# Attention with one ones-matmul for two units' row sums, and an x ring of six batches

## The chip, the cores and the metric

One core of one Trainium2 chip. The metric is device time in microseconds (us), the median over several executions. The kernel before takes about 1066 us. In its first runs its executions agreed within 0.1%, but over all rounds they lie between 1063.2 and 1068.4 us, a scatter of about 0.5%; so differences of 1 or 2 us need care. Ratios are the mean time of one kernel's fast runs over that of the other's of the same rounds, so not quite the ratio of the medians quoted beside them.

## The reference, cut to what matters

Two independent attention problems, A and B, of the same shape; their outputs are concatenated.

```python
# per problem: x (16, 144, 448), k_cache and v_cache (16, 16, 512, 256), wq (448, 4096), wo (4096, 448), bf16
q = (x @ wq).reshape(B, Sq, H, Dh).transpose(0, 2, 1, 3)
scores = einsum("bhqd,bhkd->bhqk", q, k_cache) * Dh ** -0.5
p = softmax(scores, axis=-1)
o = einsum("bhqk,bhkd->bhqd", p, v_cache)
out = o.transpose(0, 2, 1, 3).reshape(B, Sq, H * Dh) @ wo
```

A *unit* is one (problem, batch, head): 512 units, each with 144 queries and 512 keys. Units 0 to 255 are problem A, 256 to 511 problem B.

## The kernel before

The scores are kept transposed: keys lie on the partitions, queries on the free axis. So the softmax sum over the keys runs over partitions, and TensorE does it: GpSimd adds the four key blocks elementwise to a tile of 128x144, and a matmul with a 128x128 tile of ones sums that tile over its partitions and puts the sum on all 128 partitions. ScalarE turns the sum into a reciprocal as exp(-ln(sum)).

```python
def t_sum(U):                                  # every unit
    t.matmul(ot_ps[ob][:, 2*SQ:3*SQ], lhsT=ones[:, :], rhs=ps_sb[:, U % NPS, :], start=True, stop=True)
def t_recip(U):
    a.activation(ln, ot_ps[ob][:, 2*SQ:3*SQ], AF.Ln)
    a.activation(rinv_sb[:, sl, :], ln, AF.Exp, scale=-1.0)
def t_check(U):                                # a guard: max and min of the sums
    v.tensor_reduce(run_sb[0:1, k, j:j+1], ot_ps[ob][0:1, 2*SQ:3*SQ], ...)   # k = max, min
# ... (cut)
# one step i of the program; every engine gets its instructions in this order
t_q(i + LQ); t_evac_q(i + LQ)    # Q projection of a unit ahead (often two batches in one), copied by VectorE
t_s(i + LS)                      # scores; ScalarE's exponentials
t_pv(i); t_sum(i)                # P.V and the ones-matmul
t_presum(i + LS)                 # GpSimd's adds
t_recip(i); t_check(i)
t_evac_ot(i)                     # VectorE: P.V times reciprocal -> ring
# ... output projection pieces ("OP"), two matmuls of 448 columns at a time
```

Every load is issued by one queue (SyncE), in a fixed order: V two units at a time into nine slots, K sixteen units at a time by a transposing DMA into two slots ("K block 16" is units 256 to 271), x by a transposing DMA. The first 48 units take their K in natural layout and are transposed by TensorE, with the old sum form in both kernels.

Of the kernel before, what the change touches and what calls it, by code (L numbers as in the profile page):

```python
# [752 lines left out]
def bass_concat_heads__mha_block_cached__gqa_block_cached__near_ridge_kernel(  # L753
# [22 lines left out]
    NP = 2  # L776
# [16 lines left out]
    LQ, LS, LT = 3, 2, 4  # L793
    KW, KR = 16, 32
    NV, NXG = 9, 2
    NNAT = 3 * KW // UV
    assert KR % KW == 0 and NU % KW == 0
    XB = 4
    assert Bn % (NXG * XB) == 0 and H == KW
    NQT, NPT, NPS, NRI, NOST, NRUN = 11, 3, 2, 2, 2, 32  # L800
# [3 lines left out]
    NXGT = NP * Bn // XB  # L804
# [12 lines left out]
    with contextlib.ExitStack() as es:  # L817
# [13 lines left out]
        xt_sb = sb("xt_sb", [128, 4, NXG * XB * SQ], BF16)  # L831
# [6 lines left out]
        run_sb = sb("run_sb", [1, 2, NRUN], BF16)  # L838
        runs_sb = sb("runs_sb", [1, 2, NT // NRUN], F32)
# [17 lines left out]
        for i in range(NXG):  # L857
            sem_names.append("xt%d" % i)
# [8 lines left out]
        def unit(U):  # L867
            pr, r = divmod(U, NU)
            b, h = divmod(r, H)
            return pr, b, h  # L870

# [43 lines left out]
        def t_load_x(XG):  # L915
            pr, j = divmod(XG, Bn // XB)
            sl = XG % NXG
            c0 = sl * XB * SQ
            x = xs[pr][j * XB:(j + 1) * XB].rearrange("b q d -> (b q) d")

            def e(q):
                q.dma_start_transpose(xt_sb[:, 0:3, c0:c0 + XB * SQ], x[:, 0:384]).then_inc(sems["xt%d" % sl], 16)  # L922
                return q.dma_start_transpose(xt_sb[:, 3, c0:c0 + XB * SQ], x[:, 320:448]).then_inc(sems["xt%d" % sl], 16)  # L923
            S.add(SP, e, writes=[(("xt", sl), XG)], dma_sem="xt%d" % sl, n_dma=2, name="x%d" % XG)
# [59 lines left out]
        def q_pair(U):  # L984

            b, h = unit(U)[1:]
            if U < NNAT * UV:
                return 1
            if U < NNAT * UV + H and h % 2 == 0:
                return 1  # L990
            if h % 2 == 0:
                return 2 if b % 2 == 0 else 0
            j = b % (NXG * XB)
            return 1 if j in (0, NXG * XB - 1) else (2 if j % 2 else 0)
# [3 lines left out]
        for U in range(NT):  # L998
            for u in [u for u in q_live if u - LS < U - LQ]:
                del q_live[u]  # L1000
            free = [k for k in range(NQT) if k not in q_live.values()][:q_pair(U)]
            for k, sl in enumerate(free):
                q_slot[U + k * H] = q_live[U + k * H] = sl

        def t_q(U):
            pr, b, h = unit(U)
            n = q_pair(U)
            xo = b % (NXG * XB) * SQ
            xr = sorted(set((pr * Bn + b + k) // XB for k in range(n)))
            hg = h // 4  # L1010

            def e(t):
                ins = None
                for dc in range(2):
                    for kc in range(4):
                        c0 = h * DH + dc * 128
                        acc = qp_ps[:, dc, 0:2 * SQ] if n == 2 else qp_ps[:, 0, dc * SQ:(dc + 1) * SQ]
                        ins = t.matmul(acc, lhsT=wq_sb[:, kc, c0:c0 + 128],  # L1018
                                       rhs=xt_sb[:, kc, xo:xo + n * SQ], start=(kc == 0), stop=(kc == 3))
                return ins  # L1020
            S.add(PE, e, reads=[(("wq", hg), pr), ("wqz", 0)] + [(("xt", XG % NXG), XG) for XG in xr],
                  writes=[(bk, ("q", U)) for bk in q_banks[:n]], banks=q_banks[:n], name="Q%d" % U)

        def t_evac_q(U):
            n = q_pair(U)
            us = [U + k * H for k in range(n)]
            a, b = q_slot[us[0]], q_slot[us[-1]]

            def e(v):
                if n == 1:  # L1030
                    return v.tensor_copy(qt_sb[:, a, :, :], qp_ps[:, 0, 0:2 * SQ].rearrange("p (e q) -> p e q", e=2))  # L1031
                return v.tensor_copy(qt_sb[:, a:b + 1:b - a, :, :],  # L1032
                                     qp_ps[:, :, 0:2 * SQ].rearrange("p e (u q) -> p u e q", u=2))
            S.add(DVE, e, reads=[(bk, ("q", U)) for bk in q_banks[:n]],
                  writes=[(("qt", q_slot[u]), u) for u in us], banks=q_banks[:n],
                  name="eq%d" % U)

        def t_s(U):
# [4 lines left out]
            kn = [(("ktn", U % KR), U)] if U < NNAT * UV else []  # L1043
            psl = U % NPT
            for k in range(2):
                bank = k if U < NNAT * UV else (2 * U + k) % 3
# [11 lines left out]
            for k in range(2):  # L1058
                bank = k if U < NNAT * UV else (2 * U + k) % 3

                def x(a, k=k, bank=bank):
                    return a.activation(pt_sb[:, psl, 2 * k:2 * k + 2, :].rearrange("p b q -> p (b q)"),  # L1062
                                        s_ps[bank][:, 0:2 * SQ], AF.Exp, scale=DH ** -0.5)
                S.add(ACT, x, reads=[(("sp", bank), 2 * U + k)], writes=[(("pt", psl), U)], banks=["s%d" % bank],
                      name="ex%d.%d" % (U, k))

        def t_presum(U):
# [5 lines left out]
            S.add(POOL, e1, reads=[(("pt", psl), U)], writes=[("pp", U)], name="pp%d" % U)  # L1073

            def e2(g):
                return g.tensor_tensor(ps_sb[:, sl, :], pp_sb[:, 0, :], pp_sb[:, 1, :], op=ALU.add)  # L1076
            S.add(POOL, e2, reads=[("pp", U)], writes=[(("ps", sl), U)], name="ps%d" % U)
# [26 lines left out]
        def t_sum(U):  # L1104
            sl = U % NPS
            ob = U % 2

            def e(t):
                return t.matmul(ot_ps[ob][:, 2 * SQ:3 * SQ], lhsT=ones[:, :], rhs=ps_sb[:, sl, :],  # L1109
                                start=True, stop=True)  # L1110
            S.add(PE, e, reads=[("ones", 0), (("ps", sl), U)], writes=[(("sum", ob), U)],
                  banks=["ot%d" % ob], name="SM%d" % U)

        def t_recip(U):
            ob = U % 2
            sl = U % NRI
            ln = rinv_sb[:, sl, :]

            def e1(a):
                return a.activation(ln, ot_ps[ob][:, 2 * SQ:3 * SQ], AF.Ln)  # L1120
            S.add(ACT, e1, reads=[(("sum", ob), U)], writes=[(("rinv", sl), (U, 0))], banks=["ot%d" % ob],
                  name="ln%d" % U)

            def e2(a):
                return a.activation(rinv_sb[:, sl, :], ln, AF.Exp, scale=-1.0)  # L1125
            S.add(ACT, e2, reads=[(("rinv", sl), (U, 0))], writes=[(("rinv", sl), U)], name="rc%d" % U)
# [22 lines left out]
        def t_check(U):  # L1149
            ob = U % 2  # L1150
            j = U % NRUN
            for k, op in ((0, ALU.max), (1, ALU.min)):
                def e(v, k=k, op=op):
                    return v.tensor_reduce(run_sb[0:1, k, j:j + 1], ot_ps[ob][0:1, 2 * SQ:3 * SQ], axis=AX.X, op=op)  # L1154
                S.add(DVE, e, reads=[(("sum", ob), U)], writes=[(("run", k), U // NRUN)], banks=["ot%d" % ob],
                      name="ck%d.%d" % (U, k))
            if j == NRUN - 1:
                for k, op in ((0, ALU.max), (1, ALU.min)):
                    def e(v, k=k, op=op):
                        return v.tensor_reduce(runs_sb[0:1, k, U // NRUN:U // NRUN + 1], run_sb[0:1, k, :],  # L1160
                                               axis=AX.X, op=op)
                    S.add(DVE, e, reads=[(("run", k), U // NRUN)], writes=[(("runs", k), 0)],
                          name="cr%d.%d" % (U, k))

        def t_flag():
            for k, op in ((0, ALU.max), (1, ALU.min)):
                def e1(v, k=k, op=op):
                    return v.tensor_reduce(stat[0:1, 2 + k:3 + k], runs_sb[0:1, k, :], axis=AX.X, op=op)
                S.add(DVE, e1, reads=[(("runs", k), 0)], writes=[(("runx", k), 0)], name="runx%d" % k)

            def e2(v):
                return v.tensor_scalar(stat[0:1, 1:2], stat[0:1, 2:3], 2.0 ** LIM_EXP, None, op0=ALU.is_gt)
            S.add(DVE, e2, reads=[(("runx", 0), 0), ("scr1", 0)], writes=[("fl0", 0)], name="fl0")

            def e3(v):
                return v.scalar_tensor_tensor(flag_sb[0:1, 0:1], stat[0:1, 3:4], 2.0 ** -LIM_EXP, stat[0:1, 1:2],
                                              op0=ALU.is_lt, op1=ALU.max)
            return S.add(DVE, e3, reads=[(("runx", 1), 0), ("fl0", 0)], writes=[("flag", 0)], name="flag")
# [51 lines left out]
        s_min = -LQ - 24  # L1230
# [7 lines left out]

        for XG in range(1, NXGT):
            lo = (XG - NXG + 1) * XB * H - LQ if XG >= NXG else s_min  # L1240
            plan(lo, 0, t_load_x, XG)
        for W in range(NNAT * UV // KW, NKW):
            plan(KW * (W + 1) - KR - LS, 1, t_load_k, W)
# [21 lines left out]
        for fn, args in dma_plan:  # L1265
# [5 lines left out]
            elif fn is t_load_k:  # L1271
                lo = KW * (args[0] + 1) - KR - LS
            elif fn is t_load_x and args[0] >= NXG:
                lo = (args[0] - NXG + 1) * XB * H - LQ
            elif fn is t_load_wq and args[0]:
                lo = NU - H + 4 * args[1] + 4 - LQ
# [5 lines left out]
        qp_free = NT - LQ  # L1282
# [22 lines left out]
        while True:  # L1305
# [13 lines left out]
            if 0 <= u < NNAT * UV:  # L1319
                t_tr(u, 0)  # L1320
            u = i + LQ
            if 0 <= u < NT and q_pair(u):
                t_q(u)
                t_evac_q(u)
            u = i + LS
            if 0 <= u < NT:
                t_s(u)
            u = i + LT
            if 0 <= u < NNAT * UV:
                t_tr(u, 1)  # L1330
            if -LS <= i < 0:
                t_presum(i + LS)
            u = i
            if 0 <= u < NT:
                t_pv(u)
                t_sum(u)
                if u + LS < NT:
                    t_presum(u + LS)
                t_recip(u)
                t_check(u)  # L1340
# [42 lines left out]
        flag_ap = flag_sb[0:1, 0:1]  # L1383
# [72 lines left out]
```

## Time and profile before

1066.05 us (1065.64 to 1066.07, three runs). The profile is of another execution, which took 1063.18 us, 2.9 us less than that median; its span is 1061.4 us.

From the page of the kernel before: busy time, three of the rows of 40 slices, and the chain of work that ended last.

```profile
PE 1043.1 (98%) x12736; PEld 895.5 (84%) x12736; DVE 670.9 (63%) x2063; ACT 706.4 (67%) x2133; POOL 625.6 (59%) x1030
...
PE   6999999999999999999998999999999999999997
...
PEclk9999999999999999999998999999999999999999
DMA  9999999999999999999999999999999999999950
...
PE 97%; DMA 2%; SPq 1%; DVE 0%; issue 0%; ACT 0%; DVEq 0%
```

TensorE (PE) is busy nearly throughout and makes up 97% of the chain.

The groups that the change touches, by line and shape: busy us and mean ns of one, then the idle time of the engine just before them.

```profile
L1109 PE MATMUL ot_ps<-ps_sb,ones 128*128 128x144 bf16 x512 | 115.9, 226 | 0.0
...
L1154 DVE TENSOR_REDUCE run_sb<-ot_ps 1x1 bf16<-1x144 f32 x1024 | 262.3, 293 | 324.0 <-ACT rinv_sb L1120 324.0
...
L1120 ACT ACTIVATE rinv_sb<-ot_ps 128x144 f32<-128x144 f32 x512 | 150.1, 293 | 51.0 <-PE ot_ps L1109 8.0
...
L1125 ACT ACTIVATE rinv_sb<-rinv_sb 128x144 f32<-128x144 f32 x512 | 165.4, 323 | 16.1
```

A matmul's 226 ns is the length of its record, not its price. The price is the distance between starts, 62.5 ns here. Part of TensorE's timeline in mid-run (start us, duration, line, count):

```profile
501.27 1.14 PE L1018 MATMUL qp_ps<-xt_sb,wq_sb 128*128 128x288 bf16 x8
502.25 0.66 PE L1052 MATMUL s_ps<-qt_sb,kt_sb 128*128 128x144 bf16 x8
502.75 0.66 PE L1097 MATMUL ot_ps<-pt_sb,v_sb 128*128 128x144 bf16 x8
503.25 0.23 PE L1109 MATMUL ot_ps<-ps_sb,ones 128*128 128x144 bf16 x1
503.31 0.54 PE L1196 MATMUL op_ps<-wo_sb,ring 128*128 128x448 bf16 x2
```

Eight matmuls of 144 columns take 502.75 - 502.25 = 0.50 us, 62.5 ns each; the ones-matmul 0.06 us; eight of 288 columns 0.98 us. Over the whole trace the typical distances are 63, 123 and 189 ns for 144, 288 and 448 columns (56 ns for 128); columns/2.4 + 2.5 ns is a straight line fitted to them. This gives a yardstick: **lost time** is the sum, over successive matmuls, of the distance between starts beyond columns/2.4 + 2.5 ns (gaps of 8 ns or less are left out). Because a matmul is shown as 226 ns long but may be followed after 62 ns, a gap of up to 160 ns doesn't show as idle time at all; lost time sees it.

Who TensorE waited for, longest in total first (us in total, times, longest):

```profile
PE s_ps L972 <- DMA v_sb<-in_A_k_cache_dram: 6.1, 4, 4.7
PE qp_ps L1018 <- DMA xt_sb<-in_A_x_dram: 3.6, 1, 3.6
PE ot_ps L1097 <- DMA v_sb<-in_B_v_cache_dram: 3.0, 1, 3.0
PE op_ps L1196 <- DVE ring L1140: 0.4, 1, 0.4
```

The first two are the start, the third is one wait for V at the switch from A to B.

### The profile page before, as it was taken

To read this page: it belongs to the slowest core of one execution; us is meant where nothing else is said; L and a number is where in the kernel's file an instruction comes from. 1 tells how busy PE (TensorE), PEld (TensorE's weight loads), DVE (VectorE), ACT (ScalarE), POOL (GpSimd) and SP (SyncE) were. 2 spreads that over 40 slices of the span, in tenths; PEclk is the share of its full clock that TensorE was granted. 3 is DMA by queue.
4 is the path that set the end of the run, shared out by engine and by line. 5 is a ranking of instruction groups with operands and counts; after the bars stand their busy time and mean duration, and the time that the engine had idled before them with its cause. 6 is when DMAs were issued, how large, how long until landed. Compare 5 with 4: busy or idle time off the path is not lost.

```text
span 1061.4 us, 32383 instructions
## 1 busy us (share of the span) xinstructions
PE 1043.1 (98%) x12736; PEld 895.5 (84%) x12736; DVE 670.9 (63%) x2063; ACT 706.4 (67%) x2133; POOL 625.6 (59%) x1030
## 2 busy tenths in 40 slices
PE   6999999999999999999998999999999999999997
PEld 6999888888888888888887888888888888888885
DVE  4776666666666666666665666666666666666664
ACT  4887656667756666666855666676775666667674
POOL 3554555656656566666754656566665555666663
PEclk9999999999999999999998999999999999999999
DMA  9999999999999999999999999999999999999950
GB/s 304 379 350 285 295 293 254 274 297 273 292 276 298 208 280 267 290 292 298 262 287 352 265 274 290 291 290 301 264 263 265 304 285 289 289 290 279 239 187 13
DMA packets 588801, 294.15 MB, mean 277 GB/s; under 512 B 500576, under 2 KB 513376, under 8 KB 588640
## 3 DMA queue, kind: packets, MB, share of 16 engines
q1 hardware_dynamic: 588640, 291.99, 109.1%
q8 instruction: 102, 1.67, 0.6%
q14 instruction: 59, 0.48, 0.2%
HBM read 161.48 MB, written 4.13 MB: 156 GB/s over the span
## 4 chain that ended last, share of the span: by engine, by line
PE 97%; DMA 2%; SPq 1%; DVE 0%; issue 0%; ACT 0%; DVEq 0%
PE s_ps L1052 24%; PE ot_ps L1097 24%; PE qp_ps L1018 24%; PE op_ps L1196 20%; PE ot_ps L1109 3%; DMA v_sb<-in_A_k_cache_dram 1%; PE s_ps L972 1%; PE qp_ps L972 1%; PE qp_ps L1196 1%; DMA v_sb<-in_B_v_cache_dram 1%; SPq L922 0%; SPq L923 0%; DVE ost_sb L1217 0%; SPq L902 0%; DVE run_sb L1154 0%
## 5 line engine op out<-in xcount | busy, mean ns | idle before, releaser
L1072 POOL TENSOR_TENSOR pp_sb<-pt_sb 128x288 f32<-128x288 bf16 x512 | 374.0, 731 | 345.7 <-ACT pt_sb L1062 323.5
L1062 ACT ACTIVATE pt_sb<-s_ps 128x288 bf16<-128x288 f32 x1024 | 364.4, 408 | 268.5 <-PE s_ps L1052 268.0
L1154 DVE TENSOR_REDUCE run_sb<-ot_ps 1x1 bf16<-1x144 f32 x1024 | 262.3, 293 | 324.0 <-ACT rinv_sb L1120 324.0
L1097 PE MATMUL ot_ps<-pt_sb,v_sb 128*128 128x144 bf16 x4096 | 340.7, 226 | 3.0 <-DMA v_sb<-in_B_v_cache_dram 3.0
L1052 PE MATMUL s_ps<-qt_sb,kt_sb 128*128 128x144 bf16 x4096 | 340.8, 226 | 0.0
L1052 PEld LDWEIGHTS s_ps<-qt_sb,kt_sb 128*128 128x128 bf16 x4096 | 288.2, 98 | 43.5 <-DVE qt_sb L1032 0.2
L1018 PE MATMUL qp_ps<-xt_sb,wq_sb 128*128 128x288 bf16 (+1 forms) x2496 | 305.3, 266 | 3.6 <-DMA xt_sb<-in_A_x_dram 3.6
L1076 POOL TENSOR_TENSOR ps_sb<-pp_sb 128x144 bf16<-128x144 f32 x512 | 250.8, 490 | 76.2 <-PE ot_ps L1109 3.1
L1018 PEld LDWEIGHTS qp_ps<-xt_sb,wq_sb 128*128 128x128 bf16 x2496 | 218.8, 98 | 79.0 <-issue 4.4
L1196 PE MATMUL op_ps<-wo_sb,ring 128*128 128x448 bf16 x1120 | 285.0, 353 | 0.4 <-DVE ring L1140 0.4
L1097 PEld LDWEIGHTS ot_ps<-pt_sb,v_sb 128*128 128x128 bf16 x4096 | 274.6, 98 | 3.7 <-DMA v_sb<-in_B_v_cache_dram 3.2
L1140 DVE TENSOR_TENSOR ring<-ot_ps,rinv_sb 128x288 bf16<-128x288 f32 (+2 forms) x640 | 231.0, 375 | 0.0
L1120 ACT ACTIVATE rinv_sb<-ot_ps 128x144 f32<-128x144 f32 x512 | 150.1, 293 | 51.0 <-PE ot_ps L1109 8.0
L1032 DVE CAST qt_sb<-qp_ps 128x576 bf16<-128x576 f32 x200 | 151.1, 755 | 41.7 <-PE qp_ps L1018 37.6
L1125 ACT ACTIVATE rinv_sb<-rinv_sb 128x144 f32<-128x144 f32 x512 | 165.4, 323 | 16.1
L1109 PE MATMUL ot_ps<-ps_sb,ones 128*128 128x144 bf16 x512 | 115.9, 226 | 0.0
L1196 PEld LDWEIGHTS op_ps<-wo_sb,ring 128*128 128x128 bf16 x1120 | 94.0, 98 | 21.8 <-DVE ring L1140 0.8
L1031 DVE CAST qt_sb<-qp_ps 128x288 bf16<-128x288 f32 x112 | 49.2, 439 | 9.4 <-PE qp_ps L1018 8.8
L1109 PEld LDWEIGHTS ot_ps<-ps_sb,ones 128*128 128x128 bf16 x512 | 50.2, 98 | 0.0
L980 ACT ACTIVATE kt_sb<-qp_ps 128x512 bf16<-128x512 bf16 x48 | 28.9, 603 | 8.5 <-PE qp_ps L972 8.5
L972 PE MATMUL s_ps<-qt_sb,v_sb 128*128 128x128 bf16 x192 | 19.4, 226 | 6.2 <-DMA v_sb<-in_A_k_cache_dram 6.1
L980 DVE COPY kt_sb<-s_ps 128x512 bf16<-128x512 bf16 x48 | 19.5, 405 | 6.3 <-PE s_ps L972 6.2
(21 smaller groups left out, 85.1 us busy)
## 6 DMA issues: line engine op xcount, KB each, us to landing
v_sb<-in_A_v_cache_dram SPq DMA_DIRECT2D x128, 512.0 KB, 6.9
v_sb<-in_B_v_cache_dram SPq DMA_DIRECT2D x128, 512.0 KB, 7.1
v_sb<-in_A_k_cache_dram SPq DMA_DIRECT2D x24, 512.0 KB, 9.3
out_dram<-ost_sb SPq DMA_DIRECT2D x36, 112.0 KB, 6.1
wo_sb<-in_A_wo_dram SPq DMA_DIRECT2D x8, 448.0 KB, 8.5
wo_sb<-in_B_wo_dram SPq DMA_DIRECT2D x8, 448.0 KB, 8.9
wq_sb<-in_A_wq_dram SPq DMA_DIRECT2D x4, 768.0 KB, 9.2
wq_sb<-in_B_wq_dram SPq DMA_DIRECT2D x4, 768.0 KB, 10.1
```

Source lines behind the costliest of these rows:

```text
L1018: ins = t.matmul(acc, lhsT=wq_sb[:, kc, c0:c0 + 128], rhs=xt_sb[:, kc, xo:xo + n * SQ], start=(kc == 0), stop=(kc == 3))
L1032: return v.tensor_copy(qt_sb[:, a:b + 1:b - a, :, :], qp_ps[:, :, 0:2 * SQ].rearrange("p e (u q) -> p u e q", u=2))
L1052: ins = t.matmul(s_ps[bank][:, (c % 2) * SQ:(c % 2 + 1) * SQ], lhsT=kt_sb[:, 2 * c + dc, ko:ko + 128], rhs=qt_sb[:, qsl, dc, :], start=(dc ...
L1062: return a.activation(pt_sb[:, psl, 2 * k:2 * k + 2, :].rearrange("p b q -> p (b q)"), s_ps[bank][:, 0:2 * SQ], AF.Exp, scale=DH ** -0.5)
L1072: return g.tensor_tensor(pp_sb[:, :, :], pt_sb[:, psl, 0:2, :], pt_sb[:, psl, 2:4, :], op=ALU.add)
L1076: return g.tensor_tensor(ps_sb[:, sl, :], pp_sb[:, 0, :], pp_sb[:, 1, :], op=ALU.add)
L1097: ins = t.matmul(ot_ps[ob][:, dc * SQ:(dc + 1) * SQ], lhsT=v_sb[:, vsl, j, c * DH + dc * 128:c * DH + (dc + 1) * 128], rhs=pt_sb[:, sl, c, ...
L1109: return t.matmul(ot_ps[ob][:, 2 * SQ:3 * SQ], lhsT=ones[:, :], rhs=ps_sb[:, sl, :], start=True, stop=True)
L1125: return a.activation(rinv_sb[:, sl, :], ln, AF.Exp, scale=-1.0)
L1140: ins = v.tensor_tensor(ring[:, 2 * h:2 * h + 2, r0:r0 + q1 - q0], ot_ps[ob][:, 0:2 * SQ].rearrange("p (c q) -> p c q", c=2)[:, :, q0:q1], ...
L1154: return v.tensor_reduce(run_sb[0:1, k, j:j + 1], ot_ps[ob][0:1, 2 * SQ:3 * SQ], axis=AX.X, op=op)
L1196: ins = t.matmul(acc[0:m, 0:D], lhsT=ring[:, c, col0:col0 + m], rhs=wo_sb[:, c, :], start=(c == first), stop=(c == last))
```

## The change

The intent: fewer columns on TensorE. After GpSimd's adds, VectorE adds partitions 0 to 63 and 64 to 127 of a unit's tile. Even units' halves go to partitions 0 to 63 of a shared tile, odd units' to 64 to 127. The ones tile becomes block-diagonal, so one matmul sums both units. Of the 464 units after the first 48, 232 ones-matmuls go. ScalarE takes one Ln for both, but runs two half-height exponentials per unit to spread each unit's reciprocal over all partitions. To give the longer path time, scores lead by three units and not two, with four probability buffers and not three; the space comes from an x ring of six batches and not eight. The ring is loaded in smaller groups (the first has two batches, not four), and lets batches 7 and 8 be projected as a pair.

The core of the diff (cut: guard arithmetic, assertions, the loading plan for x, the choice of slots):

```diff
-    LQ, LS, LT = 3, 2, 4
+    LT = 4
-    NV, NXG = 9, 2
+    NV, NX = 9, 6
+    X_GROUPS = ((0, 2), (2, 6), (6, 10), (10, 14), (14, 18), (18, 20), (20, 24), (24, 28), (28, 32))
-    NQT, NPT, NPS, NRI, NOST, NRUN = 11, 3, 2, 2, 2, 32
+    NQT, NPT, NPS, NRI, NOST, NRUN = 11, 4, 2, 2, 2, 28
+    P0 = NNAT * UV                                   # 48
+        def ls(U):
+            return 2 if U < P0 else 3
+        def lq(U):
+            return ls(U) + 1
+        def t_pair_ones():
+                g.memset(ones[0:64, 64:128], 0.0)
+                return g.memset(ones[64:128, 0:64], 0.0)
+        def t_halves(U):
+            sl = U // 2 % NPS
+            p0 = U % 2 * 64
+                return v.tensor_tensor(ps_sb[p0:p0 + 64, sl, :], p2_sb[0:64, :], p2_sb[64:128, :], op=ALU.add)
...
+            h0 = U % 2 * 64                           # t_recip from unit 48 on
+            for p0 in (0, 64):
+                    return a.activation(rinv_sb[p0:p0 + 64, sl, :], ln_sb[h0:h0 + 64, :], AF.Exp, scale=-1.0)
...
+            if P0 <= u < NT and u % 2:
+                t_recip(u)
             if 0 <= u < NT:
                 t_pv(u)
-                t_sum(u)
+                if u < P0 or u % 2 == 0:
+                    t_sum(u)
+            if P0 <= u + 2 < NT:
+                t_halves(u + 2)
```

## The prediction

> **What bounds the kernel now.** TensorE. The chain that ended last is 97% PE (DMA 2%); PE is busy 98% of the 1061.4 us span, VectorE 63%, ScalarE 67%, GpSimd 59%. In the windows table PE is busy throughout from 60 to 1000 us, except 3.1 us near 561 us (a wait for the V load at the switch to problem B). Otherwise PE idles in the first 14 us (3.6 us for x, 4.7 us for K) and the last few. In the timeline matmuls follow each other at the pace of their columns: eight of 144 columns every 0.50 us (62.5 ns each), a ones-matmul 0.06 us, a paired projection 0.98 us, a single one 0.50 us. So time is columns streamed, plus start, tail and one DMA wait.
>
> **What is removed on PE.** The first 48 units keep the old form; the other 464 share ones-matmuls two by two: 232 x 62.5 ns = 14.5 us go, all on the chain. The six-batch ring cuts single projections from 112 to 80, giving 16 more pairs, but pairing saves only 1.00 - 0.98 = 0.02 us each: 0.3 us.
>
> **Start and tail.** x0 is two batches, not four. Its two transposes hold the queue for 3.6 + 1.9 us before the second K load, and the first projection waits for them until 9.96 us. Halved, that is up to 2.7 us earlier; other first loads may then bind, so I count 1.8 us. The last (odd) unit has its reciprocal before its PV: about 0.6 us off the tail.
>
> **What is added elsewhere.** VectorE: 464 half-adds of 64x144 fp32. [...] 464 reduces go (293 ns each, -136 us). [...] ScalarE: 232 Ln go (-68 us), 464 more exponentials come (323 ns for 144 columns[...]): +150 us, so ~790 us, 75%. GpSimd unchanged, ~625 us. None reaches PE: the extra exponential lengthens the release of an even unit's bank by ~0.3 us, but that bank is needed two units (4 us) later; scores lead by three units. The closest margin: the next projection's copy waits behind that release, with about 0.3-0.5 us before its scores. [...] x loads come ~16 units (32 us) ahead of use rather than 64; they land in ~6 us. I allow +1.5 us for small stalls, the hand-over at unit 48 and the unchanged V wait.
>
> **Sum.** 1066.05 - 14.5 - 0.3 - 1.8 - 0.6 + 1.5 = about 1050.4 us (-1.5%). Range 1046 to 1057. Faster by over 2% 0.06, within 2% 0.92, slower 0.02.
>
> **What would show it.** Ones-matmul count 280; PE still 97% of the chain, busy about 15 us less; no new PE waits over 5 us in total mid-run; first projection near 8 us; ScalarE busy ~790 us[...].
>
> **What would make it wrong.** PE waiting on VectorE [...], on ScalarE, or on x with its shorter lead; a longer V wait; a start gaining nothing. Over 2% needs the V wait gone and the start gaining fully.

ScalarE's +150 us is the author's estimate: 464 times the 323 ns that the profile before shows at 128 partitions.

## More of the kernel before

At the switch from A to B the weights wq and wo (about 7 MB) are loaded again; the order there is written out by hand:

```python
MID = ("k16 v127 v128 q0 v129 v130 q1 v131 q2 q3 v132 k17 v133 v134 v135 v136 v137 o0 o1 v138 o2 v139 o3 v140 o4 v141 "
       "o5 v142 o6 o7 k18")
```

## The result, and the profile after

1056.19 us (1055.05 to 1058.97, four runs) against 1066.06 us: ratio 0.9911, 95% interval 0.9889 to 0.9932. The output is correct. The time lies in the range, but the gain is 9.9 us where 15.6 was predicted.

The page of the changed kernel, the same parts:

```profile
PE 1031.0 (98%) x12376; PEld 875.0 (83%) x12376; DVE 740.9 (70%) x2039; ACT 793.9 (75%) x2365; POOL 636.6 (60%) x1030
...
PE 91%; DMA 5%; ACT 1%; DVE 1%; SPq 1%; issue 0%; POOL 0%; ACTq 0%; DVEq 0%
```

PE's share of the chain fell from 97% to 91%; DMA, ACT and DVE came in. The groups that answer to those of before:

```profile
L1120 DVE TENSOR_TENSOR ps_sb<-p_sb 64x144 bf16<-64x144 f32 x464 | 158.7, 342 | 44.4 <-POOL p_sb L1111 30.3
L1209 DVE TENSOR_REDUCE run_sb<-ot_ps 128x1 bf16<-128x144 f32 x560 | 146.5, 304 | 79.4 <-ACT ln_sb L1166 44.3 <-ACT rinv_sb L1166 31.0
...
L1179 ACT ACTIVATE rinv_sb<-ln_sb 64x144 f32<-64x144 f32 x928 | 298.3, 321 | 24.3
...
L1158 PE MATMUL ot_ps<-ps_sb,ones 128*128 128x144 bf16 x280 | 63.4, 226 | 0.0
```

The counts are as intended: 280 ones-matmuls, 464 half-adds, 928 exponentials. An exponential of 64 partitions takes as long (321 ns) as one of 128 did (323 ns), so halving the partitions saved nothing here, while the one of 128x288 elements takes 408 ns. The waits of TensorE:

```profile
PE s_ps L1000 <- DMA v_sb<-in_A_k_cache_dram: 6.3, 4, 4.7
PE qp_ps L1052 <- DMA wq_sb<-in_B_wq_dram: 3.6, 1, 3.6
PE s_ps L1086 <- DMA kt_sb<-in_B_k_cache_dram: 2.9, 1, 2.9
PE qp_ps L1052 <- DMA xt_sb<-in_A_x_dram: 2.3, 1, 2.3
PE s_ps L1086 <- DVE qt_sb L1066: 1.5, 5, 0.4
PE s_ps L1000 <- DVE run_sb L1209: 0.8, 1, 0.8
PE qp_ps L1052 <- DVE qt_sb L1065: 0.6, 1, 0.6
PE s_ps L1086 <- ACT pt_sb L1096: 0.3, 1, 0.3
```

There are two kinds of new wait: for loads of problem B (wq and K, 6.5 us, where before it was 3.0 us for V), and for VectorE's projection copy (qt_sb, 2.1 us). With lost time, the whole difference between the two profiled spans can be split by stage:

```text
us                                     before    after   difference
columns (sum of columns/2.4 + 2.5 ns)  1035.2   1020.3     -14.8
up to the first matmul                    4.7      4.7       0.0
lost time   0 to  60 us (start)           9.0      8.0      -1.0
lost time  60 to 135 us (unit 48)         0.0      1.4      +1.4
lost time 135 to 490 us                   0.0      1.0      +1.0
lost time 490 to 650 us (switch)          6.5     12.3      +5.8
lost time 650 us on                       0.5      1.5      +0.9
from the last matmul's start              5.5      6.2      +0.6
span                                   1061.4   1055.3      -6.1
```

The columns fell by exactly what was predicted. The other rows need care: the profiled execution of the changed kernel was one of the slower of its four (1057.08 us), that of the kernel before a fast one (1063.18 us), so the two spans differ by 6.1 us and not by 9.9. In a second profile of the changed kernel (e4 below) the switch lost 10.3 us and the span was 1052.0 us. The table points to the switch, but how much of the shortfall lies there it cannot tell; e2 and e3 can.

TensorE's timeline there, in the changed kernel; brackets give the idle time and what ended it:

```profile
526.06 0.54 PE L1259 MATMUL op_ps<-wo_sb,ring 128*128 128x448 bf16 x2
530.18 1.39 PE L1052 MATMUL qp_ps<-xt_sb,wq_sb 128*128 128x288 bf16 x8 [3.58 <-DMA wq_sb<-in_B_wq_dram]
531.37 1.17 PE L1086 MATMUL s_ps<-qt_sb,kt_sb 128*128 128x144 bf16 x8
532.33 1.17 PE L1142 MATMUL ot_ps<-pt_sb,v_sb 128*128 128x144 bf16 x8
...
535.25 0.66 PE L1142 MATMUL ot_ps<-pt_sb,v_sb 128*128 128x144 bf16 x8
```

And in the kernel before:

```profile
566.88 1.14 PE L1097 MATMUL ot_ps<-pt_sb,v_sb 128*128 128x144 bf16 x8 [3.05 <-DMA v_sb<-in_B_v_cache_dram]
...
573.54 0.66 PE L1052 MATMUL s_ps<-qt_sb,kt_sb 128*128 128x144 bf16 x8
```

After the 3.58 us wait, eight matmuls of 144 columns take 0.96 us, not 0.50: the trace's clock record has TensorE at half speed (0.5) for 3.41 us from 530.9 us on, 0.75 us after the wait's end, and again for 3.41 us from 606.0 us, 1.1 us after the end of the wait of 2.91 us for K. In the kernel before, 6.83 us at half speed begin at 565.9 us, 1.0 us before the wait of 3.05 us for V ends. In e5 below, waits of 7.4 and 4.4 us came with 6.8 and 3.4 us at half clock; in e4 a wait of 2.6 us was followed by none, and in e9, where no wait at the switch was longer than 2.1 us, there was none. What decides when the half clock sets in was not shown.

### The profile page after: what moved, and what is told of

Read it like the earlier page. It is cut to its first block, busy times and chain, and to the rows that moved or that the text cites. A ratio compares the mean times of both kernels' runs of the same rounds, so it can differ in the third digit from the quotient of the medians.

```text
span 1055.3 us, 32320 instructions
## 1 busy us (share of the span) xinstructions
PE 1031.0 (98%) x12376; PEld 875.0 (83%) x12376; DVE 740.9 (70%) x2039; ACT 793.9 (75%) x2365; POOL 636.6 (60%) x1030
## 4 chain that ended last, share of the span: by engine, by line
PE 91%; DMA 5%; ACT 1%; DVE 1%; SPq 1%; issue 0%; POOL 0%; ACTq 0%; DVEq 0%
PE s_ps L1086 23%; PE ot_ps L1142 23%; PE qp_ps L1052 22%; PE op_ps L1259 19%; DMA kt_sb<-in_B_k_cache_dram 2%; DMA v_sb<-in_A_k_cache_dram 2%; PE ot_ps L1158 2%; PE s_ps L1000 1%; PE qp_ps L1000 1%; DMA wq_sb<-in_B_wq_dram 1%; PE qp_ps L1259 1%; ACT rinv_sb L1179 0%; ACT pt_sb L1096 0%; DVE ring L1194 0%; DVE qt_sb L1066 0%
## 5 line engine op out<-in xcount | busy, mean ns | idle before, releaser
L1194 DVE TENSOR_TENSOR ring<-ot_ps,rinv_sb 128x288 bf16<-128x288 f32 (+2 forms) x640 | 241.9, 394 | 150.3 <-ACT rinv_sb L1179 145.8
L1086 PE MATMUL s_ps<-qt_sb,kt_sb 128*128 128x144 bf16 x4096 | 341.3, 226 | 4.7 <-DMA kt_sb<-in_B_k_cache_dram 2.9
L1086 PEld LDWEIGHTS s_ps<-qt_sb,kt_sb 128*128 128x128 bf16 x4096 | 287.7, 98 | 56.9 <-DVE qt_sb L1066 5.6
L1179 ACT ACTIVATE rinv_sb<-ln_sb 64x144 f32<-64x144 f32 x928 | 298.3, 321 | 24.3
L1111 POOL TENSOR_TENSOR p_sb<-pp_sb 128x144 f32<-128x144 f32 x464 | 227.5, 490 | 74.6 <-DVE ps_sb L1120 10.4
L1209 DVE TENSOR_REDUCE run_sb<-ot_ps 128x1 bf16<-128x144 f32 x560 | 146.5, 304 | 79.4 <-ACT ln_sb L1166 44.3
L1120 DVE TENSOR_TENSOR ps_sb<-p_sb 64x144 bf16<-64x144 f32 x464 | 158.7, 342 | 44.4 <-POOL p_sb L1111 30.3
L1066 DVE CAST qt_sb<-qp_ps 128x576 bf16<-128x576 f32 x216 | 162.1, 751 | 21.3 <-PE qp_ps L1052 17.7
L1166 ACT ACTIVATE ln_sb<-ot_ps 128x144 f32<-128x144 f32 x232 | 67.9, 293 | 32.6 <-PE ot_ps L1158 25.3
L1158 PE MATMUL ot_ps<-ps_sb,ones 128*128 128x144 bf16 x280 | 63.4, 226 | 0.0
L1065 DVE CAST qt_sb<-qp_ps 128x288 bf16<-128x288 f32 x80 | 35.9, 448 | 4.8 <-PE qp_ps L1052 4.3
L1111 POOL TENSOR_TENSOR ps_sb<-pp_sb 128x144 bf16<-128x144 f32 x48 | 23.5, 490 | 6.9 <-PE ot_ps L1158 0.3
L1158 PEld LDWEIGHTS ot_ps<-ps_sb,ones 128*128 128x128 bf16 x280 | 27.5, 98 | 0.0
```

The lines of the kernel that those rows point to most:

```text
L1066: return v.tensor_copy(qt_sb[:, a:b + 1:b - a, :, :], qp_ps[:, :, 0:2 * SQ].rearrange("p e (u q) -> p u e q", u=2))
L1086: ins = t.matmul(s_ps[bank][:, (c % 2) * SQ:(c % 2 + 1) * SQ], lhsT=kt_sb[:, 2 * c + dc, ko:ko + 128], rhs=qt_sb[:, qsl, dc, :], start=(dc ...
L1111: return g.tensor_tensor(dst, pp_sb[:, 0, :], pp_sb[:, 1, :], op=ALU.add)
L1120: return v.tensor_tensor(ps_sb[p0:p0 + 64, sl, :], p2_sb[0:64, :], p2_sb[64:128, :], op=ALU.add)
L1179: return a.activation(rinv_sb[p0:p0 + 64, sl, :], ln_sb[h0:h0 + 64, :], AF.Exp, scale=-1.0)
L1194: ins = v.tensor_tensor(ring[:, 2 * h:2 * h + 2, r0:r0 + q1 - q0], ot_ps[ob][:, 0:2 * SQ].rearrange("p (c q) -> p c q", c=2)[:, :, q0:q1], ...
```

## The experiments

Theory DMA: the loads are served in one stream that has little slack; at the switch 7 MB of weights are added to it; TensorE, having become faster, meets the stream there and gets only part of its gain. Theory ENGINES: the missing 5 to 6 us are waits for the added work on VectorE and ScalarE.

### e1: the columns out, nothing put in

The kernel before, odd units after 48 without their own sum (wrong result; it passed the comparison all the same, presumably as neighbouring heads have nearly the same row sums).

```diff
+                own = u < P0 or u % 2 == 0
+                if own:
-                t_sum(u)
+                    t_sum(u)
+                if own:
-                t_recip(u)
-                t_check(u)
+                    t_recip(u)
+                    t_check(u)
# evacuation of an odd unit reads the even unit's reciprocal
```

> The kernel before with 232 ones-matmuls taken out and nothing put in: from unit 48 on, odd units have no ones-matmul, Ln, exponential or check and use the even unit's reciprocal (wrong result on purpose). TensorE has the columns of the change (14.5 us fewer), while VectorE and ScalarE each lose over 130 us of work. Theory DMA (the DMA stream at the switch from problem A to B takes its time whatever TensorE does, and eats much of the gain as waits and half-clock there): it also falls short, about 1055 us (1053 to 1057), PE idle plus slow clock between 500 and 650 us grows from about 6.5 us to 9 or more. Rival ENGINES (the missing 5 us are waits for the half-adds and extra exponentials): the full gain, 1051.5 us or less, and 500 to 650 us as in the kernel before.

Measured: 1055.13 us, ratio 0.9893 (0.9876 to 0.991), a gain of 10.8 us. (By the ratio it is 11.4 us.) Lost time from 490 to 650 us is 11.7 us, and 0.2 us from 135 to 490 us; one more wait for V, 1.45 us, comes at 792 us. So with no added work at all and 232 fewer matmuls, 3 to 4 us of the 14.5 are missing, mostly at the switch. That part cannot come from the half-adds or the exponentials. It does not follow that the changed kernel loses as much to DMA: its engine waits delay it on the way to the switch.

### e2 and e3: both kernels without the reload of the weights

B uses A's weights (wrong result).

```diff
-    MID = ("k16 v127 v128 q0 v129 v130 q1 v131 q2 q3 v132 k17 ... o6 o7 k18")
+    MID = ("k16 v127 v128 v129 v130 v131 v132 k17 ... v142 k18")
-            reads=[(("wq", hg), pr), ...                   # and wo alike
+            reads=[(("wq", hg), 0), ...
```

> The kernel before, but the weights of problem B are not loaded; B uses A's (wrong result on purpose). 7 MB fall out of the DMA stream at the switch. Both theories: the V wait near 561 us and the half-clock after it vanish, 5.5 to 6.5 us less than before: about 1060 us. It is the base for the next run.

> The changed kernel with the weights of B not loaded (wrong result on purpose). Theory DMA: both waits of the switch (for wq and for K) and the half-clock after each vanish, 11 to 12 us less than the changed kernel, about 1044.5 us; against the kernel before without reload the full 14 to 16 us. Rival ENGINES: the change is worth 10 us here as well, so about 1050 us.

Measured: 1057.21 us (0.9921) and 1046.06 us (0.9816). e2 gained more than expected: 8.4 us by the ratio, 8.7 by the medians, where the profile of the kernel before shows 6.5 us lost at the switch (again, it was a fast execution). All longer waits of TensorE in e3 (the first two lines are the start):

```profile
PE s_ps L1000 <- DMA v_sb<-in_A_k_cache_dram: 5.7, 3, 4.7
PE qp_ps L1052 <- DMA xt_sb<-in_A_x_dram: 2.5, 1, 2.5
PE s_ps L1086 <- DVE qt_sb L1066: 1.5, 5, 0.4
PE qp_ps L1052 <- DVE qt_sb L1065: 0.6, 1, 0.6
PE s_ps L1086 <- ACT pt_sb L1096: 0.3, 1, 0.3
```

The waits for B's loads are gone, as expected. But the change is worth 0.9816/0.9921 = 0.9894 here, 11.2 us, not the 14 to 16 that theory DMA asked for. So theory DMA alone falls: the waits for VectorE are still there. Split like the first pair (spans 1055.5 and 1043.9): columns -14.8, start -2.2, unit 48 +1.4, 135 to 490 us +1.0, 490 to 650 us +1.8, after 650 us +0.9, end +0.4. That is 5.1 us lost to engines without any DMA in it. The reload itself costs the kernel before 8.4 to 8.7 us, and the changed one 9.8 to 9.9 us (e3 against e4 below): about 1.5 us or less of the change's gain goes to DMA, which the scatter of the runs does not set apart from nothing for certain. So the larger part of the shortfall is engines. Without the reload the executions of either kernel lie within 1.2 us of each other, so most of the scatter comes with the reload.

### e4: the changed kernel again

> The changed kernel unaltered, on the same chip as the three runs above, for the scatter of its time and of the place of its waits. Theory DMA: 1055 to 1059 us, waits for DMA of 5 to 8 us between 500 and 650 us, perhaps for other loads than in the first profile (V, wq or K), since whichever load comes last is chance. ENGINES: the same time, waits in the middle the same as before.

Measured: 1055.87 us (1053.52 to 1057.75, six runs), ratio 0.9909. Its waits were again for wq (3.5 us) and K (2.6 us), so the places seem not to be chance; a half-clock stretch followed only the first (mean granted clock 0.997, against 0.996 in the first profile). The losses at unit 48, from 135 to 490 us and after 650 us are the same as in the first profile within 0.02 us: those are built into the program's order.

### e5 and e6: the projection's copy first

Where are the small waits? In the changed kernel near 315 us, TensorE's timeline and then VectorE's:

```profile
315.17 0.66 PE L1142 MATMUL ot_ps<-pt_sb,v_sb 128*128 128x144 bf16 x8
316.07 0.67 PE L1086 MATMUL s_ps<-qt_sb,kt_sb 128*128 128x144 bf16 x8 [0.23 <-DVE qt_sb L1066]
```

```profile
314.90 0.44 DVE L1194 TENSOR_TENSOR ring<-ot_ps,rinv_sb 128x288 bf16<-128x288 f32 x1
315.27 0.74 DVE L1066 CAST qt_sb<-qp_ps 128x576 bf16<-128x576 f32 x1
```

The copy of the projection (L1066) starts only when the even unit's evacuation (L1194) is through, and that waited for Ln and two exponentials; the scores (L1086) wait for the copy. It costs 0.4 us here (0.90 us between the two starts, not 0.50), in a step without output-projection pieces to fill the time. e5 puts the evacuation behind the copy; e6 does so without the reload.

```diff
                 if q_pair(u):
                     t_q(u)
                     t_evac_q(u)
+            while held:
+                t_evac_ot(held.pop())
...
-                t_evac_ot(u)
+                if u >= P0 and u % 2 == 0 and any(q_pair(w) for w in of_step(lq, i + 1)):
+                    held.append(u)
+                else:
+                    t_evac_ot(u)
```

> The changed kernel; only VectorE's order differs: where the next step has a projection, an even unit's output evacuation (which waits for Ln and two exponentials) is queued behind that projection's copy instead of ahead of it. Theory COPY (the small TensorE waits for the projection copy come from the copy queueing behind that evacuation): in the profile the waits of S for the copy between 135 and 490 us (1.0 us) and after 650 us (1.5 us) fall to near zero and the 1.6 us near 570 us too; the time falls by 2 to 4 us against the changed kernel, less than the waits taken away, as the DMA wait at the switch grows in exchange: 1052 to 1055 us. Rival (the copy itself, or the half-add ahead of it, is too slow): the waits stay.

> The same order of VectorE in the changed kernel without the reload of the weights (wrong result on purpose), so that DMA cannot hide it. Theory COPY: 1046.1 less about 3.5 us, about 1042.5 us, leaving the 1.4 us at the hand-over at unit 48. Against the kernel before without reload that is -14.7 us, the full worth of the removed matmuls and no more than 2 us beside. Rival: 1046 us as without the order.

Measured e6: 1044.37 us (0.9794, and 0.9794/0.9816 = 0.9978 of e3): 1.7 us gained by the medians, 2.4 by the ratios, where 3.5 were expected. The line for L1066 is gone from the waits. Lost time went from 1.0 to 0.65 us (135 to 490 us), 2.2 to 1.0 (490 to 650) and 1.5 to 0.7 (after 650). What stays are gaps of 0.09 to 0.17 us, next to ends of ScalarE's exponentials and of half-adds. That is 2.2 us of lost time gone, of the 3.7 that the change had added there: theory COPY is right for somewhat over half of these losses.

Measured e5, with the reload: 1060.40 us (1059.13 to 1060.86), ratio 0.9948. It is 4 us *slower* than the changed kernel, the opposite of what was expected. Its waits for the copy are gone as in e6, yet the switch lost 17.0 us:

```profile
PE qp_ps L1052 <- DMA wq_sb<-in_B_wq_dram: 7.4, 1, 7.4
...
PE s_ps L1086 <- DMA kt_sb<-in_B_k_cache_dram: 4.4, 1, 4.4
```

Removing engine waits made TensorE reach the first projection of B earlier (525.3 us, against 526.6 in the first profile of the changed kernel) and wait longer there, and on top of it wq landed later (the projection started at 532.8 us, against 530.2). From the landing of K block 16 to that of K block 18 took 83.0 us, against 80.4 and 79.9 us in the two profiles of the changed kernel. Why the stream ran 3 us longer stays open.

### e7, e8 and e12: other orders of loads at the switch

e7 puts the first wq block ahead of K block 16 and K block 18 ahead of half of wo; e8 is e7 with the copy first; e12 puts all of wo behind K block 18. All three also start B's output projection later, by 8 or 10 units.

```diff
 # e7, e8
-    MID = ("k16 v127 v128 q0 v129 ... o3 v140 o4 v141 o5 v142 o6 o7 k18")
+    MID = ("v127 v128 q0 k16 v129 ... o3 v140 v141 v142 k18 o4 o5 o6 o7")
-    OP_DELAY, OP_START, OP_START_B = 2, 28, 20
+    OP_DELAY, OP_START, OP_START_B = 2, 28, 28
 # e12
+    MID = ("k16 v127 v128 q0 v129 ... v137 v138 v139 v140 v141 v142 k18 o0 o1 o2 o3 o4 o5 o6 o7")
+    OP_DELAY, OP_START, OP_START_B = 2, 28, 30
```

> The changed kernel with another order of loads at the switch: the first wq block of B ahead of the K block that held it up, K block 18 ahead of half of wo, and B's output projection starting 8 units later. Theory DMA: the wait for wq (3.6 us plus half clock 1.7 us) becomes a shorter one (0 to 2 us) and the wait for K block 18 shrinks; 2 to 5 us less than the changed kernel, 1051 to 1054 us, and some risk that the wait only moves to another load (then 1055 us).

> Both: VectorE's order and the order of loads. If both theories hold and the DMA stream has room: 1049 to 1052 us, better than both kernels. If the DMA stream at the switch is the bound in any order: no better than the run with the order of loads alone.

> The changed kernel; at the switch all of wo is loaded after K block 18, whose landing has so far set when TensorE goes on (604.8 us, and the end 449 to 451 us later in five profiles), and B's output projection starts 10 units later. K block 18 should land about 10 us earlier, near 594 us, and its wait goes. Theory DMA (the stream as a whole, not one load, is what TensorE meets): the wait moves to K block 19, which lands no earlier than the 636 us of the changed kernel by more than 2 us, and the gain is small: 1053 to 1057 us. Rival (K block 18 alone was the obstacle): the whole wait and half clock, about 5 us, are gained: 1050 to 1052 us.

Measured: e7 1062.55 us (0.9962), e8 1060.43 us (0.9952), e12 1063.20 us (0.9976). All are slower than the changed kernel, and e7 and e12 missed every time that had been expected of them. K block 18 did land earlier (601.7, 601.2 and 597.9 us, against 604.8), but the waits moved: in e7 to V (7.5 us in two waits), in e8 to K blocks 16, 18 and 19, in e12 to wq (7.5 us) and V (6.0 us). Starting B's output projection later may also have taken away work that TensorE could have done while waiting; no run separates this from the order of loads. Advancing one load moved the wait to others. e8 came out 2 us better than e7, with overlapping intervals.

### e9 and e10: is it the half clock?

Matmuls of ones times ones, whose results are overwritten, ahead of the first projection of B and of the scores of unit 288. They keep TensorE active during the waits.

```diff
+        def t_fill(n, acc, key, bank):
+                for _k in range(n):
+                    ins = t.matmul(acc[:, 0:128], lhsT=ones[:, :], rhs=ones[:, :], start=True, stop=True)
+                    if u == NU:                       # before t_q; e9: 50, e10: 110
+                        t_fill(50, qp_ps[:, 0, :], "qp", "qp")
+                if u == NU + KR:                      # before t_s; e9: 36, e10: 64
+                    t_fill(36, s_ps[2 * u % 3], ("sp", 2 * u % 3), "s%d" % (2 * u % 3))
```

> The changed kernel with idle matmuls (ones times ones, results overwritten) ahead of the two places where TensorE stood idle for a load at the switch: 50 before the first projection of B (about 2.8 us of the 3.6 us wait) and 36 before the scores of unit 288 (about 2.0 us of 2.9 us). Nothing useful is added. Theory HALF CLOCK (each idle of about 3 us at the switch is followed by 3.4 us or more at half clock, which costs 1.7 us or more beside the wait): no half-clock stretch in mid-run, 1.7 to 3.4 us less than the changed kernel, 1052.5 to 1054.5 us. Rival (the half clock costs nothing, the loads are late anyway): the same time as the changed kernel, 1056 us, or more.

> The run with the copy first (1060.4 us, waits of 7.4 and 4.4 us at the switch, 6.8 + 3.4 us at half clock) with such idle matmuls for 6.2 and 3.6 us at the two places. If its 4 us loss against the changed kernel comes of the half clock: about 5 us less, 1055 to 1056 us. If it comes of loads that land later: at most 2 us less.

Measured e9: 1056.84 us (0.9916): no gain. Of the waits in its profile at the switch:

```profile
PE s_ps L1095 <- DMA kt_sb<-in_B_k_cache_dram: 2.5, 2, 2.1
PE qp_ps L1061 <- DMA wq_sb<-in_B_wq_dram: 1.7, 1, 1.7
...
PE ot_ps L1151 <- DMA v_sb<-in_B_v_cache_dram: 0.8, 1, 0.8
```

The clock record shows no half-clock stretch in mid-run (mean granted clock 1.0 over the execution and 1.00 from 490 to 650 us, against 0.996 and 0.98 in the first profile of the changed kernel), so the fillers did what they should, and it was worth nothing: the loads landed no earlier (K block 19 at 638.4 us, used at 638.5), so the time won by the full clock went into waiting (2.1 us of it for K block 18). Theory HALF CLOCK falls for the changed kernel. e10: 1058.44 us (0.9934), 2 us less than e5. That is the "at most 2 us" of loads that land later, not the 5 us of the half clock.

### e11: one V load beside each K block

```diff
+                if fn is t_load_k:
+                    beside = 1
+                if fn is t_load_v and beside:
+                    beside -= 1
+                    fn(*args, eng=ACT)               # issued by ScalarE
+                else:
-                fn(*args)
+                    fn(*args)
```

> The changed kernel; only the first V load after each K block is issued by ScalarE instead of the queue's own engine, so that it moves beside the K block and not behind it. If the switch is bound by the order in which one queue serves its loads: the waits for V and wq shrink, 1051 to 1054 us. If it is bound by what the DMA engines move in total, as theory DMA has it: K lands later by what V took, and the time stays within 2 us of 1056 us; it is longer if the issuing delays ScalarE's exponentials.

Measured: 1073.95 us, the median of six runs, one of which (1083.19 us) counts as slow; the five fast ones took 1066.54 to 1078.73 us, median 1072.56. The ratio is 1.0096: slower than the kernel before, and outside both expectations. In its profile, that of its fastest run, K blocks landed 3 us later than in the changed kernel at first and 6 to 17 us later from the third on, TensorE waited 9.7 us for wq, and for K in problem A (2.9 us in four waits) where no other kernel did. ScalarE's groups were as long as in the changed kernel (exponentials 408 and 321 ns, Ln 293 ns). A second issuing engine brought no load in sooner. The run does not tell why the stream became longer and not just reordered.

### The stream and TensorE side by side

This table shows where the stream and TensorE meet. It gives the landing of K block 19 (units 304 to 319), the start of the scores of unit 304, which need it, and the time from there to the end of the span, all in us from the traces.

```text
run                        K19 landed  S(304) starts  from there to the end
before                         639.8       640.7            420.7
changed                        636.3       638.6            416.7
e4  changed again              634.8       635.7            416.3
e1  odd sums skipped           636.4       638.2            415.4
e9  fillers                    638.4       638.5            416.6
e5  copy first                 642.2       642.4            416.3
e10 copy first, fillers        642.2       642.3            415.6
e7  switch order               640.8       642.6            419.7
e8  both                       638.5       638.7            420.2
e12 wo last                    641.0       643.0            421.0
without reload:
e2  before                     622.9       635.0            420.5
e3  changed                    616.1       627.5            416.5
e6  changed, copy first        619.0       626.6            416.3
```

With the reload, unit 304 starts 0.1 to 2.3 us after its K block has landed, in every run of the table, the kernel before included. Without the reload the block is there 7.6 to 12.1 us ahead, and TensorE's own pace shows. After unit 304 the changed kernel always needs about 416 us (the runs that start B's output projection later have more of it left).

The slack was small all along. A K block occupies the stream for about 17.2 us in these traces (from the landing before it to its own), and V loads that follow each other closely land 1.35 us apart: an estimate from these is 17.2 + 8 x 1.35 = 28.0 us per sixteen units, before x and the stores. Sixteen units take TensorE about 31.9 us before and 31.5 after (scores of unit 64 to 240 over eleven blocks). K blocks landed every 31.7 us in both kernels (block 4 to block 15). K block 15 was 11.3 us ahead of its use before, 6.5 us after. It would be easy to say that TensorE, now faster, ate up the lead, but e1 speaks against it: with the same columns and the old buffers its K blocks landed every 31.2 us, and block 15 was 10.3 us ahead. And block 16, the last before the burst of weights, was 8.7 us ahead before, 10.4 after and 12.4 in e1. What hardly moves is the burst: from the landing of block 16 to that of block 18 it takes 80.0 us before, 80.4 and 79.9 in the changed kernel and 79.9 in e1, and 64.5 and 57.5 without the reload (e2, e3).

## Why the prediction was right or wrong, point by point

- **Columns on TensorE, 14.5 + 0.3 us: right.** The traces have 14.8 us fewer.
- **Start, 1.8 us: about right.** Lost time in the first 60 us fell by 1.0 and 2.2 us in the two matched pairs. The first projection started at 8.7 and 9.2 us in the two profiles of the changed kernel, not 9.96.
- **Tail, 0.6 us: the wait went, the sum didn't move.** The 0.5 us that the last output projection waited in the kernel before is gone; the time from the last matmul's start to the end was 0.4 to 0.6 us longer in the matched pairs. One look each does not separate that from scatter of the last stores.
- **"I allow +1.5 us for small stalls, the hand-over at unit 48 and the unchanged V wait": this is the term that failed.** The hand-over alone was 1.4 us. The waits for copies, exponentials and half-adds were 3.7 us (e2 and e3, where no DMA hides them). Together 5.1 us, 3.6 more than allowed. And the reload cost 1.1 to 1.5 us more than in the kernel before. With the tail (1.0 us worse than predicted in e2 and e3) and the start (0.4 us better) this makes up 5.3 to 5.7 us, and 15.6 - 9.9 = 5.7 us were missing. (The profiles show 5.8 and 3.7 us more lost at the switch, but against a fast execution of the kernel before.)
- **"None reaches PE": wrong, at the place that it named itself.** The copy behind the evacuation was called the closest margin, "0.3-0.5 us before its scores". In steps without output-projection pieces that margin is gone. e6 recovered about 2 us by changing that order. Two checks that the prediction had set itself failed with it: PE's share of the chain fell to 91% and did not stay at 97%, and the new waits in mid-run were 8.9 us in total and not under 5.
- **ScalarE about 790 us: right (793.9).** Its estimate took 323 ns for a half-height exponential; 321 ns were measured. VectorE went from 670.9 to 740.9 us. The reduces run in overlapping pairs (two records of about 0.30 us within 0.51 us), so that taking 464 away saved 116 us of busy time and not 136. The half-adds added 159 us: 422 of them took 300 to 310 ns, and 42, all begun inside a first add of GpSimd, 457 to 881 ns. The rest is evacuations 11 us longer in total and less overlap between VectorE's instructions.
- **The longer queue of x with a shorter lead: no harm.** No wait for x after the start in any profile.
- **A half-clock stretch after a wait** was not in the prediction; e9 shows that avoiding it would have gained nothing (1056.84 against 1056.19 us).
- **Why the total was in the range:** it had room for an unspecified loss of 6.6 us beyond the 1050.4, and the time lay 0.8 us inside its upper edge. The width of the range held it, not the account of what the added work costs; that part is luck. What it also did not have was the reading that DMA, at 9 in nearly all slices and with 0.9 us of slack at K block 19, stood right behind TensorE at the switch, where the repair of the engines' order did not pay out (e5).

What stays open: why the stream takes 3 us longer at the switch with the copy first, why K block 15 has less lead in the changed kernel than in e1 (the x ring and its order of loads differ too, and no run isolates them), and whether a gain is possible at the switch without more buffers. No kernel with right results tried here beats the changed one; six other orders of its work (e5, e7, e8, e10, e11, e12) were slower and the fillers (e9) the same.

## What to carry to other kernels

Before costing a saving on the busiest engine, follow the work that replaces it through the order of the other engines: here one evacuation ahead of one copy was worth about 2 us. And measure how far ahead of its use each load lands, block by block: where that lead is a few per cent of a block's time (0.9 of 32 us at K block 19), part of the saving may be spent waiting, and the chain of waits will not say so beforehand. Here the two met at the reload in mid-run. And a loss that one experiment removes (half clock, one late load, one engine wait) need not be a gain: look at what waits next before believing it.

## What the traces showed of single operations

- The half-add of 64x144 fp32 on VectorE: 422 of 464 took 300 to 310 ns to the nearest ten (changed kernel).
- Half-adds and GpSimd's first adds (changed kernel): all 42 slow half-adds had begun inside a first add and ended 0.16 us after it, whether they began 16 or 435 ns into it. In the other direction, a first add that began inside a half-add stayed at about 0.73 us where the two overlapped by up to 0.12 us, took 0.785 us at 0.18 to 0.20 us of overlap and 0.89 us at 0.30 (spans on GpSimd are rough).
- Loads: the packets of a K block moved at 290 GB/s while they flowed (changed kernel, 322 to 329 us); with the start and the pauses a block of 4.19 MB in 17.2 us is 244 GB/s. V loads of 512 KB landing 1.35 us apart are 388 GB/s.
